# Tying the loads of the next tile's token blocks to the products on PE in a fused attention and FFN kernel

## The chip, the cores and the metric

The kernel runs on one core of a Trainium2 chip. The metric is the device time of one execution in microseconds. Five engines work in parallel, each through its own instruction list in order: PE (matrix products; its weight loads are shown as PEld), DVE and ACT (elementwise work), POOL (elementwise work too), and SP, which here only issues DMA transfers (SPq is its queue in the profile).

## The reference

```python
def reference(**kwargs):                       # B=4, H=8, S=576, D=64
    ...
    attn_out = _attn_ref(**attn_kwargs)        # softmax(q k_lm) Z softmax(q_lm k) v, 32 landmarks
    x = np.ascontiguousarray(attn_out.transpose(0, 2, 1, 3)).reshape(B * S, H * D)
    x = _moe_ref(x=x, **moe_kwargs)
    return _moe2_ref(x=x, **moe2_kwargs)

def _moe_ref(x, w_in, w_out):                  # 2304 x 512 -> 2048 -> 512
    h = x @ w_in
    relu6 = np.clip(h + 3.0, 0.0, 6.0)
    return (h * relu6 / 6.0 @ w_out).astype(np.float32)

def _moe2_ref(x, w_in, w_out):                 # 2304 x 512 -> 2048 -> 512
    h = x @ w_in
    g = np.where(h > 0.0, h, np.exp(np.minimum(h, 0.0)) - 1.0)
    return (g @ w_out).astype(np.float32)
```

A Nyström attention gives 2304 tokens of 512 values; two feed-forward layers follow. All is float32. The kernel splits each float32 operand into a high part (a cast to fp32r) and a low part (the rest), and adds three products on PE for each product of the reference. Splitting costs a cast on ACT and a subtraction on DVE or POOL; `to_pair` (line 308) does both.

## The kernel before

**Stages.** Attention and the first layer run together, in a loop over slots (`for i in range(END, NA)`). The first layer's output goes to DRAM as `x1d` (stores `x1d<-xs`). The second layer then works on three tiles of 768 tokens. Each tile runs eight steps (`for q in range(NTT * NQ)`, line 1460; 24 steps in all, q = 0 to 23), so tile 1 is q = 8 to 15 and tile 2 is q = 16 to 23.

**A step.** One step computes two blocks of 128 hidden rows for the tile's two blocks of 384 tokens, with seven block products in place of eight (`quartet`, line 1073). Each of the seven runs six products `h<-x,wi` into one of two banks, which DVE or ACT drains (`a1`, `u2`, `y`, `u3`); behind each come five or six products `x<-w,gh` and `x<-w,gl` of the step before (`second`, line 1128), which apply the output weights. Between them stand the ELU on ACT and DVE (`elu`, line 1049; `gf`) and the split of its result into `gh` (ACT) and `gl` (DVE); `ghl` is the name of such a pair in a buffer of another kind.

**The blocks of tokens.** The seven products want seven sums and differences of the tile's token blocks, for each of two halves (`kk`). `load_x` (line 992) makes them: for each half four DMA loads of 128x384 (192 KB) from `x1d` (line 1013), then eleven subtractions, of which seven belong to a split, with seven casts on ACT. Both tiles 1 and 2 do this on POOL: 8 loads, 14 casts and 22 subtractions each. It is a generator, and the loop takes one piece of it at each of the seven block places of a step (`next(xs, None)`). It starts at step q = 4 of the tile before (`XPACE`, lines 103 and 1464): tile 1's at q = 4, tile 2's at q = 12. Nothing but data and buffers holds these loads, and the scheduler places an instruction as soon as its inputs and its place are free; in the trace tile 1's loads and subtractions run from the last slots to q = 1.

**The weights.** In tile 0, `load_in2` loads the input weights of each step as written (`wi<-wi2d`, `u<-wi2d`), makes three sums of them on DVE (`u<-u,wi` and `u<-wi,u`, four instructions for a half, eight for a step) and splits them with ACT and POOL (`wi<-wi`, `wi<-u,wi`); the result is also stored (`wi2p<-wi`), and the tiles 1 and 2 load it ready from there. `load_out2` does the like with the output weights (`w<-wo2d`, split on ACT and POOL, stored by `wo2p<-w`).

**What sets the order.** A scheduler of the framework lays the instructions of all engines out by a priority (`wanted`, line 157, the smaller first) and by its own timeline of when inputs are ready. Products of the second layer go through `bmm` (line 1031), which chains each to the one before, so their order is as written; `chain[0]` is the last one placed. `gated` (line 170) ties an instruction behind the instruction in `gate[0]` (line 168), where one is set: an edge in the scheduler's order only, with no semaphore. SP's list is one queue for all loads and stores.

Of the kernel before, what the change touches and what calls it, by code (L numbers as in the profile page):

```python
# [31 lines left out]
def nystrom_ffn_kernel(ctx: ExitStack, tc, q, k, v, w_in1, w_out1, w_in2, w_out2, out):  # L32
# [46 lines left out]
    T2 = 384  # L79
# [44 lines left out]
    def after(inst, other):  # L124

        tc.add_manual_dep(
            inst.ins, other.name, mybir.DependencyInfo(mybir.DependencyClass.NoSync, mybir.DependencyReason.DATA)
        )

    vec, act, pool, pe = InOrder(nc.vector), InOrder(nc.scalar), InOrder(nc.gpsimd), InOrder(nc.tensor)  # L130
    sp = InOrder(nc.sync, False)

    def sub(o, a, b, eng=vec):
        return eng.tensor_tensor(out=o, in0=a, in1=b, op=ALU.subtract)
# [22 lines left out]
    def wanted(s):  # L157
        tc.cur_priority = int(1000 * (s + 100))
# [9 lines left out]
    gate = [None]  # L168

    def gated(inst):  # L170
        if gate[0] is not None:
            after(inst, gate[0])
# [17 lines left out]
    x1d = dram.tile([NDM, 128, NT], F32, name="x1d")  # L190
# [59 lines left out]
    def run(gen):  # L250
        for _ in gen:
            pass
# [55 lines left out]
    def to_pair(f, h, l, eng=vec):  # L308
        act.copy(out=h, in_=f)
        sub(l, f, h.bitcast(F32), eng)  # L310
# [54 lines left out]
    def scratch(n, w):  # L365

        return room().bitcast(F32).rearrange("p n t -> p (n t)")[:, 0:n * w].rearrange("p (a n) -> p a n", a=n)
# [8 lines left out]
    def sums_out2(q):  # L376

        a, b, c, d = (spare_x(4 * q + i).rearrange("p (j n) -> p j n", j=2) for i in range(4))
        for i, y in enumerate((b, a)):
            sp.dma_start(out=y, in_=wo2d[q + i * NQ].rearrange("p (j n) -> p j n", j=2))  # L380
        yield
        sub(c[:, 0], a[:, 1], a[:, 0], pool)
        sub(c[:, 1], b[:, 1], c[:, 0], pool)
        sub(d[:, 0], b[:, 1], a[:, 1], pool)
        sub(d[:, 1], c[:, 1], b[:, 0], pool)
        yield
        for x, y in ((a, c), (b, d)):
            to_pair(y, x.bitcast(F32R), y.bitcast(F32R), pool)
        yield
        o = q % 2 * HDM  # L390
        for j, ys in enumerate(((a, c), (b, d))):
            for x, y in enumerate(ys):
                sp.dma_start(out=to2p[2 * j:2 * j + 2, q // 2, x, :, o:o + HDM].rearrange("j p n -> p j n"), in_=y)
        yield
# [37 lines left out]
    def load_out2(q):  # L432

        if q // NQ in WINO:
            load_wino2(q)
            return
        for i in range(2):
            kk = q % NQ + i * NQ
            t = w2_place()
            hl = t.bitcast(F32R)  # L440
            if q < NQ:
                l = t[:, 1, :]
                sp.dma_start(out=l, in_=wo2d[kk])
                to_pair(l, hl[:, 0, :], hl[:, 1, :], pool)
                late_out.append((wo2p[kk].rearrange("x p n -> p x n"), t))
            else:
                sp.dma_start(out=t, in_=wo2p[kk].rearrange("x p n -> p x n"))
            wo2[q, i] = hl[:, 0, :], hl[:, 1, :]

    def load_in2(q):  # L450

        stores = late_out[:]
        late_out.clear()
        for kk in range(2):
            hl = []
            for x in range(2):
                if q % 2 == 0:
                    hl.append(win[0].tile([128, 7, 128], F32, name="wi", tag=f"wi{kk}{x}"))
                else:
                    t = nat.tile([128, G, W], F32, name="wi", tag=f"n{'hl'[x]}{kk}")  # L460
                    hl.append(t.rearrange("p g w -> p (g w)")[:, 0:7 * 128].rearrange("p (a n) -> p a n", a=7))
            h, l = hl
            hr, lr = h.bitcast(F32R), l.bitcast(F32R)
            wi[q, kk] = hr, lr
            flat = [x.rearrange("p a n -> p (a n)") for x in hl]
            if q >= NQ:
                for x in range(2):
                    sp.dma_start(out=flat[x], in_=wi2p[q % NQ, kk, x])
                continue
            f = scratch(4, 128)  # L470
            sp.dma_start(out=f[:, 0], in_=wi2d[q, kk][:, 3 * 128:])
            sp.dma_start(out=flat[1][:, 0:3 * 128], in_=wi2d[q, kk][:, 0:3 * 128])
            if kk:
                for o, i in stores:
                    sp.dma_start(out=o, in_=i)
                stores = []
            vec.tensor_tensor(out=f[:, 1], in0=f[:, 0], in1=l[:, 2], op=ALU.add)
            sub(f[:, 2], f[:, 1], l[:, 0])
            sub(f[:, 3], l[:, 1], f[:, 2])
            sub(f[:, 0], l[:, 0], f[:, 0])  # L480
            act.copy(out=hr[:, 0:3], in_=l[:, 0:3])
            sub(lr[:, 0:3], l[:, 0:3], h[:, 0:3], pool)
            act.copy(out=hr[:, 3:7], in_=f)
            sub(lr[:, 3:7], f, h[:, 3:7], pool)
            for x in range(2):
                late_out.append((wi2p[q, kk, x], flat[x]))
        for o, i in stores:
            sp.dma_start(out=o, in_=i)
# [490 lines left out]
    def x_places(t, n=14):  # L979

        for i in range(n):
            if t % 2 == 0:
                x = xp[0].tile([128, 2, T2], F32, name="x2", tag=f"x2{i}")
                yield x[:, 0], x[:, 1]
            elif NS + i < len(PLACES):
                x = wop.tile([128, 2, DM], F32, name="x2", tag=PLACES[NS + i])
                yield x[:, 0, 0:T2], x[:, 1, 0:T2]
            else:
                x = nat.tile([128, G, W], F32, name="x2", tag="nl3")
                yield x[:, 0, 0:T2], x[:, 1, 0:T2]  # L990

    def load_x(t, eng):

        places = x_places(t)
        t0 = 2 * T2 * t
        for kk in range(2):
            x = [next(places) for _ in range(7)]
            h, l = [y[0] for y in x], [y[1] for y in x]

            def pair(i, f):  # L1000
                xt_t[t, kk, i] = h[i].bitcast(F32R), l[i].bitcast(F32R)
                to_pair(f, *xt_t[t, kk, i], eng)

            if t:
                f = [
                    nat.tile([128, G, HALF], F32, name="xf", tag=n).rearrange("p g t -> p (g t)")[:, 0:T2]
                    for n in ("ath0", "ath1", "atl0")
                ]
            else:
                f = scratch(2, T2)  # L1010
                f = [f[:, 0], f[:, 1], scratch(1, T2)[:, 0]]
            for o, r, c in ((f[0], 0, 1), (l[0], 0, 0), (l[2], 1, 1), (l[1], 1, 0)):
                sp.dma_start(out=o, in_=x1d[2 * r + kk, :, t0 + c * T2:t0 + c * T2 + T2])
            yield
            sub(f[1], f[0], l[0], eng)
            yield
            sub(f[0], l[2], f[0], eng)
            yield
            sub(f[2], l[2], f[1], eng)
            yield  # L1020
            pair(5, f[0])
            yield
            sub(f[0], l[1], f[2], eng)
            yield
            for i, g in ((3, f[1]), (4, f[2]), (6, f[0]), (0, l[0]), (1, l[1]), (2, l[2])):
                pair(i, g)
                yield

    chain = [None]
# [380 lines left out]
    for i in range(END, NA):  # L1410
        b, r = i // SB, i % SB
# [48 lines left out]
    for q in range(NTT * NQ):  # L1460
        wanted(NA + 4 * q - 2)
        if q:
            load_in2(q + 1) if q + 1 < NTT * NQ else None
        if q % NQ == XPACE and q // NQ + 1 < NTT:
            xs = load_x(q // NQ + 1, pool)
        steps_ = quartet(q)
        if q == (WINO[0] - 1) * NQ:
            more = (None for r in range(NQ) for _ in sums_out2(r))
        for p in range(7):
            if p == 2:  # L1470
                load_out2(q)
            wanted(NA + 4 * q + 4 * p / 7 + 4)
            if conv and p % 2 == 0:
                conv.pop(0)()
            if p == 4 and q % NQ == NQ - 2 and q // NQ in WINO:
                load_late2(q // NQ, 0)
                load_late2(q // NQ, 1)
            next(more, None)
            next(xs, None)
            wanted(NA + 4 * q + 4 * p / 7)  # L1480
            next(steps_)
            for _ in range(2):
                next(tail, None)
            while n < (7 * q + p + 1 - 7 - LAG) * 12 * NS2 // 7:
                next(behind)
                n += 1
        run(steps_)
# [37 lines left out]
```

## Time and profile before

| what | value |
|---|---|
| time, median of 3 runs | 820.44 us (818.43 to 821.87) |
| the profiled execution | 818.11 us |
| its span | 816.3 us |
| PE busy | 782.2 us, 96% of the span |
| DVE busy | 539.4 us, 66% |
| ACT busy | 465.4 us, 57% |
| POOL busy | 416.2 us, 51% |
| DMA | 226 GB/s on average |

The span is the time from the first to the last instruction in the profile; the execution's own time is 1.8 us longer. Busy times are sums over the span, and the engines overlap. A wait shown in brackets behind an instruction is the idle time of its engine just before it, and the instruction that ended it. PEclk is the granted clock of PE as a share of 2.4 GHz.

### The profile page before, as it was taken

The numbers are of one execution on the slowest core, as the hardware profiler recorded it, in microseconds if no ns is written. First come the engines' busy times: TensorE is split into PE (matmuls) and PEld (weight loads), VectorE is DVE, ScalarE is ACT, GpSimd is POOL, SyncE is SP. The second block draws the span as 40 slices with busy tenths as digits, with TensorE's granted clock in tenths as the row PEclk, the third lists the DMA queues.
The fourth block names the chain that finished last, engine by engine and source line by source line (L and its number), as shares of the span: only waits on it lengthen the run. The fifth ranks groups of instructions, "written<-read, shape, count | busy, mean of one in ns | idle before, by whom it ended". The sixth has DMA issues, their size and how long they took to land.

```text
span 816.3 us, 16233 instructions
## 1 busy us (share of the span) xinstructions
PE 782.2 (96%) x5860; PEld 695.6 (85%) x5860; DVE 539.4 (66%) x1076; ACT 465.4 (57%) x1020; POOL 416.2 (51%) x423
## 2 busy tenths in 40 slices
PE   5699989999999999999998999999999999999998
PEld 3476777688997889889998899998999889999998
DVE  7899677557645754486346766756745565777794
ACT  3587554656656656584556556646644544555562
POOL 2567566556655665455428664539662470223311
PEclk9699999999999999999999999999999999999999
DMA  9967932685577445752352477689999567867663
GB/s 323 404 189 250 311 116 71 194 270 190 199 231 260 160 143 160 244 194 101 111 197 81 169 265 259 238 305 331 386 390 344 184 223 252 275 237 256 227 195 108
DMA packets 115599, 184.56 MB, mean 226 GB/s; under 512 B 8576, under 2 KB 71552, under 8 KB 115520
## 3 DMA queue, kind: packets, MB, share of 16 engines
q1 hardware_dynamic: 115520, 183.54, 65.9%
q8 instruction: 46, 0.75, 0.4%
q14 instruction: 33, 0.27, 0.1%
HBM read 130.02 MB, written 53.48 MB: 225 GB/s over the span
## 4 chain that ended last, share of the span: by engine, by line
PE 77%; DVE 11%; DMA 5%; ACT 3%; issue 2%; POOL 1%; DVEq 0%; ACTq 0%; POOLq 0%; SPq 0%
PE x L116 40%; PE h L116 31%; PE bk L116 6%; DVE u L116 2%; DVE h L116 1%; DVE lm L116 1%; DMA kt<-in_k 1%; DVE nl L116 1%; DMA qt<-in_q 1%; DVE w1c L116 1%; DVE st L116 1%; DVE gf L116 1%; DMA w1d<-w1c 1%; DVE y L116 1%; DMA u<-in_moe_w_in 1%
## 5 line engine op out<-in xcount | busy, mean ns | idle before, releaser
L116 PE MATMUL h<-x,wi 128*128 128x384 f32 x1008 | 205.4, 339 | 0.6 <-DVE u L116 0.6
L116 PE MATMUL x<-gh,wo 128*128 128x288 f32 (+1 forms) x896 | 198.5, 297 | 0.4 <-DVE wo L116 0.3
L116 PEld LDWEIGHTS h<-x,wi 128*128 128x128 f32 x1008 | 178.9, 189 | 10.4 <-DVE u L116 1.0
L116 PEld LDWEIGHTS x<-gh,wo 128*128 128x128 f32 x896 | 149.1, 188 | 10.3 <-issue 7.2
L116 PE MATMUL x<-gl,wo 128*128 128x288 f32 (+1 forms) x448 | 130.6, 294 | 0.0
L116 POOL TENSOR_TENSOR gl<-gf,gh 128x288 fp32r<-128x288 f32 (+1 forms) x100 | 83.9, 841 | 86.3 <-ACT gh L116 69.2
L116 ACT CAST gh<-gf 128x288 fp32r<-128x288 f32 (+2 forms) x160 | 72.5, 454 | 86.2 <-DVE gf L116 85.7
L116 PE MATMUL x<-w,gh 128*128 128x512 f32 (+1 forms) x360 | 102.4, 357 | 1.0 <-ACT gh L116 1.0
L116 ACT ACTIVATE gf<-h,half_b 128x288 f32<-128x288 f32 (+2 forms) x128 | 63.7, 500 | 42.6 <-PE h L116 40.5
L116 PE MATMUL h<-atl,nh 128*128 128x288 f32 (+2 forms) x256 | 81.9, 320 | 4.6 <-DVE gf L116 2.6
L116 DVE SCALAR_TENSOR_TENSOR gf<-gf,h 128x288 f32<-128x288 f32 (+1 forms) x112 | 49.4, 442 | 54.3 <-ACT gf L116 53.5
L116 PEld LDWEIGHTS x<-gl,wo 128*128 128x128 f32 x448 | 84.2, 188 | 1.1 <-issue 0.9
L116 DVE SCALAR_TENSOR_TENSOR gf<-gf,y 128x384 f32<-128x384 f32 x80 | 61.2, 765 | 32.9 <-ACT gf L116 32.9
L116 ACT ACTIVATE gf<-y 128x384 f32<-128x384 f32 x80 | 42.0, 525 | 62.5 <-DVE y L116 62.4
L116 PE MATMUL x<-w,ghl 128*128 128x512 f32 (+1 forms) x324 | 76.6, 356 | 0.1
L116 PE MATMUL h<-ath,nl 128*128 128x288 f32 (+2 forms) x256 | 76.5, 299 | 0.0
L116 PE MATMUL h<-ath,nh 128*128 128x288 f32 (+2 forms) x256 | 76.3, 298 | 0.0
L116 PEld LDWEIGHTS x<-w,gh 128*128 128x128 f32 x360 | 65.1, 190 | 7.4 <-ACT gh L116 1.4
L116 PE MATMUL x<-w,gl 128*128 128x512 f32 (+1 forms) x180 | 64.6, 359 | 3.6 <-DVE gl L116 3.6
L116 PEld LDWEIGHTS h<-atl,nh 128*128 128x128 f32 x256 | 48.5, 190 | 17.8 <-issue 7.9
L116 POOL TENSOR_TENSOR x<-u,gf 128x384 f32<-128x384 f32 x16 | 18.1, 1151 | 84.6 <-DVE gf L116 50.9
L116 PEld LDWEIGHTS x<-w,ghl 128*128 128x128 f32 x324 | 55.2, 189 | 5.8 <-DVE ghl L116 0.3
(183 smaller groups left out, 1520.6 us busy)
## 6 DMA issues: line engine op xcount, KB each, us to landing
wi<-wi2p SPq DMA_DIRECT2D x64, 448.0 KB, 5.8
wi2p<-wi SPq DMA_DIRECT2D x32, 448.0 KB, 2.9
u<-in_moe_w_in SPq DMA_DIRECT2D x25, 512.0 KB, 4.4
w1c<-w1d SPq DMA_DIRECT2D x48, 256.0 KB, 4.5
w<-wo2p SPq DMA_DIRECT2D x24, 512.0 KB, 7.0
ub<-in_moe_w_out SPq DMA_DIRECT2D x16, 512.0 KB, 10.2
u<-in_moe_w_out SPq DMA_DIRECT2D x16, 512.0 KB, 5.6
wo2p<-w SPq DMA_DIRECT2D x16, 512.0 KB, 3.6
```

The costliest lines, as they stand in the source:

```text
L116: inst = getattr(self.eng, name)(*a, **kw)
```

## The change

The four loads of each half of a tile are passed to `gated`. The loop sets `gate[0]` to the last product placed on PE (`chain[0]`) while it takes the next piece of `load_x`, and clears it again. The first call of `load_x` (for tile 0) is taken elsewhere, with no gate, and stays as it was.

```diff
@@ -1010,7 +1010,7 @@
             for o, r, c in ((f[0], 0, 1), (l[0], 0, 0), (l[2], 1, 1), (l[1], 1, 0)):
-                sp.dma_start(out=o, in_=x1d[2 * r + kk, :, t0 + c * T2:t0 + c * T2 + T2])
+                gated(sp.dma_start(out=o, in_=x1d[2 * r + kk, :, t0 + c * T2:t0 + c * T2 + T2]))
             yield
@@ -1476,7 +1476,9 @@
             next(more, None)
+            gate[0] = chain[0]
             next(xs, None)
+            gate[0] = None
             wanted(NA + 4 * q + 4 * p / 7)
```

No instruction is added or taken away; the scheduler puts some in other places. Three places matter below.

POOL at the start of the second layer, q = 0 and 1. The names `x2_65..` and `xf_65..` are the first half of tile 1's token blocks, `x2_68..` and `xf_68..` the second; `wi_5972` and `wi_5985` are the input weights that are split for q = 2:

```order
-L116 TENSOR_TENSOR x2_6815<-xf_6820,x2_6815 128x384
-L116 TENSOR_TENSOR x2_6814<-x2_6814 128x384
 L116 TENSOR_TENSOR wi_5972<-wi_5972,wi_5971 128x384
-L116 TENSOR_TENSOR x2_6817<-xf_6819,x2_6817 128x384
+L116 TENSOR_TENSOR wi_5972<-u_5973,wi_5971 128x512
 L116 TENSOR_TENSOR wi_5985<-wi_5985,wi_5984 128x384
-L116 TENSOR_TENSOR x2_6816<-xf_6821,x2_6816 128x384
-L116 TENSOR_TENSOR wi_5972<-u_5973,wi_5971 128x512
 L116 TENSOR_TENSOR wi_5985<-u_5986,wi_5984 128x512
-L116 TENSOR_TENSOR xf_6819<-x2_6813,xf_6821 128x384
-L116 TENSOR_TENSOR x2_6813<-x2_6813 128x384
-L116 TENSOR_TENSOR x2_6818<-xf_6819,x2_6818 128x384
```

All 22 subtractions of tile 1 leave this stretch, those above and 16 ahead of them; the four of `wi` now stand in a row. On DVE nothing changes up to the first `gl` of q = 1.

SP at q = 4. `w_6374` and `w_6378` are the output weights that are split for q = 3, the `wi` loads are for q = 5:

```order
 L116 DMA wo2p<-w_6374 128x2x512
 L116 DMA wo2p<-w_6378 128x2x512
+L116 DMA xf<-x1d 128x384
+L116 DMA x_6513<-x1d 128x384
+L116 DMA x_6515<-x1d 128x384
+L116 DMA x_6514<-x1d 128x384
 L116 DMA wi<-wi2d 128x384 x2
 L116 DMA w_6558<-wo2d 128x512
```

The four loads of the first half now go between the stores of the output weights and the loads of the next input weights. The four of the second half go, one by one, between stores of weights some two steps later.

POOL at the same place, q = 4; `wi_6482` and `wi_6495` are the input weights for q = 5:

```order
 L116 TENSOR_TENSOR w2_6378<-w2_6378 128x512
+L116 TENSOR_TENSOR xf_6521<-xf_6520,x2_6513 128x384
+L116 TENSOR_TENSOR xf_6520<-x2_6515,xf_6520 128x384
+L116 TENSOR_TENSOR xf_6522<-x2_6515,xf_6521 128x384
+L116 TENSOR_TENSOR x2_6513<-x2_6513 128x384
+L116 TENSOR_TENSOR x2_6516<-xf_6521,x2_6516 128x384
 L116 TENSOR_TENSOR wi_6482<-wi_6482,wi_6481 128x384
+L116 TENSOR_TENSOR x2_6515<-x2_6515 128x384
+L116 TENSOR_TENSOR x2_6518<-xf_6520,x2_6518 128x384
 L116 TENSOR_TENSOR wi_6495<-wi_6495,wi_6494 128x384
 L116 TENSOR_TENSOR wi_6482<-u_6483,wi_6481 128x512
+L116 TENSOR_TENSOR x2_6517<-xf_6522,x2_6517 128x384
```

Five subtractions stand ahead of the splits of `wi` here, and three among them. On ACT the casts of these blocks stand among the casts and exponentials of the same step, four of them ahead of the copy `a1` that drains the step's first bank.

POOL at q = 6, for the second half:

```order
 L116 TENSOR_TENSOR w2_6745<-w2_6745 128x512
+L116 TENSOR_TENSOR xf_6820<-xf_6819,x2_6812 128x384
+L116 TENSOR_TENSOR x2_6812<-x2_6812 128x384
+L116 TENSOR_TENSOR x2_6815<-xf_6820,x2_6815 128x384
+L116 TENSOR_TENSOR xf_6819<-x2_6814,xf_6819 128x384
+L116 TENSOR_TENSOR xf_6821<-x2_6814,xf_6820 128x384
+L116 TENSOR_TENSOR x2_6814<-x2_6814 128x384
+L116 TENSOR_TENSOR x2_6817<-xf_6819,x2_6817 128x384
+L116 TENSOR_TENSOR x2_6816<-xf_6821,x2_6816 128x384
+L116 TENSOR_TENSOR xf_6819<-x2_6813,xf_6821 128x384
 L116 TENSOR_TENSOR wi_6870<-wi_6870,wi_6869 128x384
```

Nine subtractions stand in a row ahead of the splits of the input weights for the step q = 7.

## Rows read from the trace of the kernel before

**Rows 1.** Part 1 of the page: busy us, share of the span, instructions.
```profile
PE 782.2 (96%) x5860; PEld 695.6 (85%) x5860; DVE 539.4 (66%) x1076; ACT 465.4 (57%) x1020; POOL 416.2 (51%) x423
```
**Rows 2.** Waits of PE, 200 to 452, then to 700: us in total, times, longest.
```profile
PE h L116 <- DVE gf L116: 2.6, 3, 1.2
...
PE h L116 <- DVE u L116: 0.6, 1, 0.6
```
**Rows 3.** Timeline of PE, 440 to 452: start, us, instruction, idle before and releaser.
```profile
445.49 0.74 PE L116 MATMUL x<-w,gh 128*128 128x512 f32 x2 [0.99 <-ACT gh L116]
...
450.87 0.53 PE L116 MATMUL x<-w,gl 128*128 128x512 f32 x1 [3.59 <-DVE gl L116]
```
**Rows 4.** Windows: us, PE, PEld, DVE, ACT, POOL busy, PEclk, DMA share, GB/s.
```profile
350.00:400.00 50.00, 47.31 (x353) 46.39 (x352) 30.21 (x55) 30.08 (x71) 26.81 (x28) 1.00 0.37 126
400.00:430.00 30.00, 30.00 (x228) 30.00 (x227) 14.78 (x32) 16.61 (x38) 11.51 (x11) 1.00 0.58 199
452.00:454.00 2.00, 2.00 (x7) 1.81 (x7) 1.43 (x3) 1.92 (x4) 2.00 (x2) 0.50 0.35 138
454.00:456.00 2.00, 2.00 (x9) 1.73 (x8) 1.26 (x2) 0.00 (x0) 2.00 (x3) 0.73 0.23 91
```
**Rows 5.** Chain that ended last, 450 to 472: start, us, work.
```profile
450.87 1.91 PE x L116 x5
...
454.70 1.39 PE x L116 x5
...
457.15 1.14 PE x L116 x5
...
468.40 1.14 PE x L116 x5
...
470.61 1.14 PE x L116 x5
```
**Rows 6.** Timeline of DVE, 440 to 452 and 492 to 504.
```profile
444.16 1.95 DVE L116 TENSOR_TENSOR u<-u,wi 128x128 f32<-128x128 f32 x2
...
449.47 1.35 DVE L116 TENSOR_TENSOR gl<-gf,gh 128x384 fp32r<-128x384 f32 x1
...
496.10 0.48 DVE L116 TENSOR_TENSOR u<-wi,u 128x128 f32<-128x128 f32 x2
```
**Rows 7.** Groups of DVE, 442 to 452, then 476 to 556: busy us, mean ns.
```profile
L116 DVE TENSOR_TENSOR u<-u,wi 128x128 f32<-128x128 f32 x4 | 3.3, 817 | 0.1
...
L116 DVE TENSOR_TENSOR u<-u,wi 128x128 f32<-128x128 f32 x16 | 4.3, 289 | 3.7 <-DMA wi<-wi2d 3.7
```
**Rows 8.** Groups of POOL, 427 to 464: the subtractions of tile 1's blocks.
```profile
L116 POOL TENSOR_TENSOR x<-xf,x 128x384 fp32r<-128x384 f32 x8 | 9.2, 1154 | 2.6 <-DVE y L116 2.5 <-ACT x L116 0.2
L116 POOL TENSOR_TENSOR x<-x 128x384 fp32r<-128x384 f32 x6 | 6.6, 1098 | 0.2
L116 POOL TENSOR_TENSOR xf<-x,xf 128x384 f32<-128x384 f32 x6 | 6.6, 1106 | 0.2
...
L116 POOL TENSOR_TENSOR xf<-xf,x 128x384 f32<-128x384 f32 x2 | 2.4, 1223 | 11.7 <-PE h L116 9.3 <-DMA xf<-x1d 2.5
```
**Rows 9.** Timelines: ACT at 444.93, SP's queue at 488.
```profile
444.93 0.51 ACT L116 CAST gh<-gf 128x384 fp32r<-128x384 f32 x1
...
488.11 1.88 SPq L116 DMA_DIRECT2D wo2p<-w  x2
```
**Rows 10.** DMA issues: count, KB each, median us to landing.
```profile
x<-x1d SPq DMA_DIRECT2D x18, 192.0 KB, 4.7
```
**Rows 11.** Waits of POOL, 476 to 550: us in total, times, longest.
```profile
POOL wi L116 <- DVE u L116: 28.4, 4, 7.5
```
**Rows 12.** Timelines of PE and DVE, 496 to 502.
```profile
496.27 1.23 PE L116 MATMUL h<-x,wi 128*128 128x384 f32 x6
...
498.48 0.54 DVE L116 TENSOR_TENSOR u<-h,a 128x384 f32<-128x384 f32 x1
...
500.68 1.23 PE L116 MATMUL h<-x,wi 128*128 128x384 f32 x6
```

## The prediction

> **What bounds the kernel now.** I read the page first, then who waited for whom on PE, then the stretch around PE's longest wait. PE is busy 782.2 of 816.3 us [rows 1], so an edit that touches neither PE's work nor its waits costs nothing. The products on PE are the same in number. What can change is PE's waits. Between 200 us and the end the waits are few: some of up to 1.2 us on DVE [rows 2], and two close together, 0.99 us before 445.49 and 3.59 us before 450.87 [rows 3]. They lie where the loop over quartets begins (step q = 1). Behind them the granted clock fell to 0.50 and 0.73 of 2.4 GHz for two 2 us slices, while it stayed at 1.00 over the stretch that holds the waits of up to 1.2 us [rows 4]. So the clock's cost is read from the chain: x5 and the h block behind it (11 products) start 3.83 us apart from 450.87 to 454.70 and 2.45 us from there to 457.15, against 2.21 us later (468.40 to 470.61) [rows 5]. That is 1.62 + 0.24 = 1.9 us. The place costs 0.99 + 3.59 + 1.9 = 6.5 us in all, and this is the most that the change can give.
>
> Why PE waited there: the second wait is for gl, which stands on DVE behind the splits of wi (u<-u,wi and u<-wi,u). Two of these took 1.95 us from 444.16, and gl itself 1.35 us [rows 6]. The same two take 0.48 us at 496.10 [rows 6]; by groups u<-u,wi takes 817 ns on average from 442 to 452 us and 289 ns from 476 to 556 [rows 7]. What differs is POOL: from 427 to 464 us it ran the 22 subtractions of the tile 1 blocks, 9.2 + 6.6 + 6.6 + 2.4 = 24.8 us [rows 8], and each DVE split got in only between two of them. The first wait is ACT's: gh was cast at 444.93 [rows 9], behind a cast of x and one of the newly loaded wi in its queue.
>
> By the Trainium skill (SBUF — State Buffer, "Who interferes with whom") a DVE instruction with two inputs in SBUF contends with a GpSimd instruction that reads SBUF, and whoever issues first takes the shared port for its whole length while the other blocks. The trace agrees: the splits have two SBUF inputs and read 817 against 289 ns. That rule speaks against this change as much as for it, since the subtractions are only moved; what it would do at the new place is the third rival below.
>
> **The change part by part.** No instruction is added or removed, and no semaphore wait: the edge only sets the place in SP's queue. There are 16 loads, eight for each of the tiles 1 and 2.
>
> Tile 1, out of the old place. Eight loads of 192 KB leave SP's queue ahead of the first quartets, 14 casts leave ACT, 22 subtractions leave POOL. On DVE the order up to gl is the same. The wi load stays where it was, behind the third store of xs, so the splits still begin at about 444.16: I leave 0.5 us of the first wait. With POOL empty until then, two splits take 0.48 us. Ahead of gl stand seven splits and one drain of an h bank (0.54 us, as u<-h,a in [rows 12]): 444.16 + 7 x 0.24 + 0.54 = 446.4 us, and even with the 1.35 us of before gl is there at 447.7. PE comes to it at 450.87 - 3.59 = 447.28. The wait is then 0 to 0.5 us, and I leave 0.2. So 4.6 - 0.7 = 3.9 us of waits go, and without a long wait the clock should not fall: 1.9 us. Together **-5.8 us**. The next late thing would be the wi load, at 0.5 us.
>
> The PE order also changes at five steps of the last slots (an h block goes ahead of two to six products of x). PE is busy for all of 400 to 430 us [rows 4], the inputs of both are there, and I take 0.
>
> Tile 1, into the new place. The first four loads now go behind the two stores of w of q = 3, issued by 489.99 us [rows 9], and land some 4.7 us later [rows 10], just as the splits for the next quartet run (496.10 [rows 6]). POOL has room in sum: its waits for DVE in 476 to 550 us are 28.4 us [rows 11], against 24.8 us of work. But what decides is not POOL's sum, it is DVE's delay. PE has two h buffers, so the block that begins at 500.68 needs the one of 496.27 drained, and DVE drains it (u<-h,a) from 498.48 to 499.02, behind the eight splits [rows 12]. The slack is 500.68 - 499.02 = 1.66 us. A held split costs (1.95 - 0.48) / 2 = 0.74 us more. Five subtractions stand ahead of the wi work in POOL's queue; with the first under way before wi has landed, I let four splits meet them: 4 x 0.74 - 1.66 = 1.3 us, and 0.4 us for ACT, on which four of the casts now stand ahead of a1 and the exponentials, the first waiting for its DMA. That is +1.7 us at q = 4.
>
> At q = 5 three subtractions follow: 3 x 0.74 = 2.2 us, within 1.66 + 1.7 of slack (PE is already late): 0. At q = 6 nine stand in a row, and the load of wi is now behind a store that waits for POOL. In the new DVE order five splits stand ahead of the drain: 5 x 0.74 - 1.66 = 2.0 us; part of this was paid at q = 4, so I take +1.7. Bounds of these two terms together: 0 from below (28.4 us of idle POOL take all of it, the splits fall between two subtractions), and from above every split held in three quartets, 3 x (8 x 0.74 - 1.66) = 12.8 us. A gain at this place is excluded: PE does not wait at all there. I take **+3.4 us**, nearer the lower end, because the subtractions also wait for ACT's casts, and splits slip in then.
>
> Tile 2. The same loads go behind the products of q = 12 to 15. There wi comes ready from DRAM and no split runs on DVE. PE waits once between 452 and 700 us, for 0.6 us, before these loads in before [rows 2]. The second half's loads stand earlier behind the first half's, and end earlier. I take 0, up to +1.
>
> Sum: -5.8 + 3.4 = **-2.4 us**. The profiled execution took 818.11 us, span and 1.8 us around it; that gives 815.7. The median of the runs, 820.44, is 2.3 above it, so I forecast 820.44 - 2.4 = **818.0 us**. Two medians of this kernel can tell 0.5%, or 4.1 us, from no change.
>
> **The rivals.** First: the new place hides all of it (POOL's idle 28.4 us). Then -5.8: 814.6 us, 814 with the rest of the 6.5 us. For it: one sum that fits easily; against it: the first five subtractions fall on the splits by the order. Second: the old wait stays. gl remains behind the splits, which start with the wi load, and if landing and not POOL set it, only some 1 us goes and the clock falls still; with the 3.4 us: 822.8 us. Against it: the row of 1.95 us, which begins when wi has landed. That the loads do not go where the words say is ruled out by the order, so I give it no chance of its own. Third, the slower one: DVE becomes the bound at q = 4 to 6. Here all eight splits of each of three quartets are held by POOL, which runs almost without a gap (its idle time at DVE in these quartets, 28.4 us, is about the 24.8 us of the new work). The price is 12.8 - 5.8 = +7.0, 827.4 us; it is slower than before from 5.8 us of lost slack on, that is when more than six of eight splits are held in two of the three. If each stop also lets the clock fall, 1.9 us more for each.
>
> By the rule of the Trainium skill cited above (SBUF — State Buffer) this third case is what an unbroken run on POOL gives; no row shows splits beside subtractions in the steady part of the loop.
>
> **How the numbers follow.** Forecast (a loss of 1.5 to 5 us): 0.46. First rival: 0.26. Second: 0.16. Third: 0.12. The forecast's own spread is 816.3 to 819.7. The range takes in the first two rivals and the noise of the runs (818.43 to 821.87): 813.8 to 823.6. Faster by over 0.5% needs under 816.3 us: nearly all of the first rival and a sixth of the forecast, 0.30. Slower by over 0.5%, above 824.5: the third rival and a little of the second, 0.13. Within 0.5%: 0.57.
>
> **What would show it.** In the profile of the changed kernel: the splits at 444 us at some 0.28 us each; PE's wait for gl under 0.5 us, and the clock at 1.00 from 440 to 460 us; the quartet q = 2 beginning some 6 us earlier. Then xf and x subtractions on POOL from some 488 to 540 us, splits there of 0.8 us, and PE waits for u (DVE) of 1 to 2 us at the fourth h block of q = 4 and q = 6. Wrong would be the prediction if the wait for gl is still over 2 us (the load set it), if PE does not wait at all from 480 to 545 us, or if it waits there more than 6 us.

## The result and the profile after

The changed kernel takes **825.29 us** (median; 824.39 to 827.30) against 819.68 us for the kernel before on the same chips (five runs each; the 820.44 us above is the median of three of those five). The ratio is 1.0066 (95% interval 1.0044 to 1.0087): slower by some 5.6 us. 818.0 us was forecast, in a range up to 823.6; it lies outside, and on the other side of no change.

The page of the kernel after, part 1, beside [rows 1]:

```profile
PE 783.3 (95%) x5860; PEld 694.7 (84%) x5860; DVE 545.6 (66%) x1076; ACT 463.7 (56%) x1020; POOL 413.2 (50%) x423
```

PE's work is what it was; its busy time is 1.1 us longer, the span of the profile 7.2 us (823.5 against 816.3). The waits of PE in the kernel after, from 430 to 452 us and then to 700 us (us in total, times, longest), beside [rows 2, 3]:

```profile
PE x L116 <- DVE gl L116: 0.7, 1, 0.7
...
PE h L116 <- DVE u L116: 6.4, 3, 2.7
PE h L116 <- DVE y L116: 1.1, 1, 1.1
PE h L116 <- ACT a L116: 0.8, 1, 0.8
```

The 0.99 + 3.59 us of q = 1 have become 0.7. In their place stand 8.3 us at q = 4 and q = 6, all on the drains of the two h banks.

How much each step cost is read from PE's timeline: the time from the first product of a step (the first `h<-x,wi` of its seven blocks) to that of the next. From q = 9 on, the two kernels agree within 0.01 us in every step. The stretch ahead of q = 0 is left out: its end lies at 429.36 us before, at 431.68 us after, and between 428.2 and 433.1 us in the profiles of the other kernels below. The difference is there already at PE's 2400th product (273.0 us before, 275.9 after), where PE's order is still the same in both; from the 3600th product to the start of q = 1, which holds the five steps with another order on PE, PE takes 30.12 us before and 30.13 after.

| us per step | q=1 | 2 | 3 | 4 | 5 | 6 | 7 | 8 | sum against before |
|---|---|---|---|---|---|---|---|---|---|
| before | 21.00 | 15.67 | 15.63 | 15.67 | 15.63 | 15.67 | 15.63 | 16.60 | |
| after | 15.57 | 16.01 | 15.64 | 21.26 | 15.63 | 21.27 | 15.64 | 15.71 | +5.2 |

So -5.4 at q = 1, +0.3 at q = 2, **+5.6 at q = 4, +5.6 at q = 6**, -0.9 at q = 8 (of that, a wait of 0.58 us on DVE's `u`, the only one of before between 452 and 700 us, is gone). The sum is the 5.6 us of the medians to within 0.4.

**The old place** went as forecast. DVE's timeline in the kernel after, beside [rows 6]:

```profile
445.87 0.62 DVE L116 TENSOR_TENSOR u<-u,wi 128x128 f32<-128x128 f32 x2 [0.34 <-issue]
446.41 0.28 DVE L116 TENSOR_TENSOR u<-wi,u 128x128 f32<-128x128 f32 x1
...
447.92 1.36 DVE L116 TENSOR_TENSOR gl<-gf,gh 128x384 fp32r<-128x384 f32 x1
449.21 1.38 DVE L116 TENSOR_TENSOR u<-wi,u 128x128 f32<-128x128 f32 x1
```

The splits take 0.28 us while POOL is idle. At 447.83 POOL begins its own `wi` work, and `gl` and the last split take 1.36 and 1.38 us: `gl` is still held, now by work that POOL did before as well.

**The new place.** PE, DVE, ACT and POOL of the kernel after around q = 4, whose first product starts at 491.06 (start, us, instruction, idle before and releaser):

```profile
496.63 1.31 PE L116 MATMUL h<-x,wi 128*128 128x384 f32 x6 [0.78 <-ACT a L116]
...
501.83 1.91 PE L116 MATMUL h<-x,wi 128*128 128x384 f32 x6 [2.72 <-DVE u L116]
```
```profile
493.75 0.58 DVE L116 TENSOR_TENSOR ghl<-gf,ghl 128x384 fp32r<-128x384 f32 x1 [2.96 <-ACT ghl L116]
494.75 1.63 DVE L116 TENSOR_TENSOR u<-u,wi 128x128 f32<-128x128 f32 x2 [0.42 <-DMA wi<-wi2d]
496.30 1.09 DVE L116 TENSOR_TENSOR u<-wi,u 128x128 f32<-128x128 f32 x1
497.32 1.10 DVE L116 TENSOR_TENSOR u<-u,wi 128x128 f32<-128x128 f32 x1
498.35 0.28 DVE L116 TENSOR_TENSOR u<-wi,u 128x128 f32<-128x128 f32 x1
498.55 0.28 DVE L116 TENSOR_TENSOR u<-u,wi 128x128 f32<-128x128 f32 x1
498.75 1.28 DVE L116 TENSOR_TENSOR u<-wi,u 128x128 f32<-128x128 f32 x2
499.96 1.34 DVE L116 SCALAR_TENSOR_TENSOR gf<-gf,y 128x384 f32<-128x384 f32 x1
501.23 0.54 DVE L116 TENSOR_TENSOR u<-h,a 128x384 f32<-128x384 f32 x1
```
```profile
492.90 1.02 POOL L116 TENSOR_TENSOR xf<-xf,x 128x384 f32<-128x384 f32 x1 [5.78 <-DMA x<-x1d]
494.00 2.23 POOL L116 TENSOR_TENSOR xf<-x,xf 128x384 f32<-128x384 f32 x2
496.19 1.06 POOL L116 TENSOR_TENSOR x<-x 128x384 fp32r<-128x384 f32 x1
497.21 1.07 POOL L116 TENSOR_TENSOR x<-xf,x 128x384 fp32r<-128x384 f32 x1
498.86 1.03 POOL L116 TENSOR_TENSOR wi<-wi 128x384 fp32r<-128x384 f32 x1 [0.58 <-DVE u L116]
```
```profile
492.79 0.52 ACT L116 CAST x<-x 128x384 fp32r<-128x384 f32 x1 [3.06 <-DMA x<-x1d]
493.21 0.51 ACT L116 CAST ghl<-gf 128x384 fp32r<-128x384 f32 x1
...
496.12 0.46 ACT L116 COPY a<-h 128x384 f32<-128x384 f32 x1
```

DVE's timeline of the kernel before has the first split of this step, whose first product starts at 493.83:

```profile
494.80 0.29 DVE L116 TENSOR_TENSOR u<-u,wi 128x128 f32<-128x128 f32 x1 [0.72 <-DMA wi<-wi2d]
```

Read DVE's and POOL's lines side by side. Four splits run beside the five subtractions, each as long as what is left of a subtraction. In POOL's gap from 498.28 to 498.86 the next two take 0.28 us again. With the next POOL instructions the last split and `gf` are long once more. The drain `u<-h,a`, which has one operand in PSUM and one in SBUF, takes 0.54 us in all of this, as in [rows 12]; but it stands behind them, and PE waits 2.72 us for it. ACT shows the second thing: it stood 3.06 us on a cast of `x` that waited for its DMA, and `a1` came late (0.78 us on PE). The cast of `ghl` stood behind that same cast, and DVE stood 2.96 us on `ghl`, which is ahead of the splits in its list. DVE was free at 494.33 us; it then waited 0.42 us more for `wi`, which came late as well. So two things held the first split almost equally long.

The chain of the kernel after shows a third, the clock (start, us, what):

```profile
501.83 1.91 PE h L116 x6
503.74 2.12 PE x L116 x5
505.86 1.05 PE h L116 x6
506.91 1.16 PE x L116 x5
```

The block and the five products behind the wait take 4.03 us, the next ones 2.21. The granted clock was 0.58 and 0.57 in the two slices from 502 to 506 us. So q = 4 is 0.78 + 2.72 + 1.82 = 5.3 of its 5.6 us. At q = 6 PE's waits are 2.56, 1.13 and 1.09 us; the clock stays at 1.00 there.

### The profile page after: what moved, and what is told of

The parts are those of the page before. It is cut to its first block, busy times and chain, and to the rows that moved or that the text cites. A ratio compares the mean times of both kernels' runs of the same rounds, so it can differ in the third digit from the quotient of the medians.

```text
span 823.5 us, 16234 instructions
## 1 busy us (share of the span) xinstructions
PE 783.3 (95%) x5860; PEld 694.7 (84%) x5860; DVE 545.6 (66%) x1076; ACT 463.7 (56%) x1020; POOL 413.2 (50%) x423
## 4 chain that ended last, share of the span: by engine, by line
PE 64%; DVE 15%; DMA 10%; ACT 5%; issue 3%; POOL 2%; SPq 1%; DVEq 0%; ACTq 0%; POOLq 0%
PE x L116 33%; PE h L116 26%; PE bk L116 5%; DVE u L116 3%; DMA u<-in_moe_w_in 2%; DMA u<-in_moe_w_out 2%; DVE h L116 2%; DMA wi<-wi2d 1%; DVE gf L116 1%; DVE nl L116 1%; DVE w1c L116 1%; DMA kt<-in_k 1%; DVE y L116 1%; DMA x<-x1d 1%; ACT gf L116 1%
## 5 line engine op out<-in xcount | busy, mean ns | idle before, releaser
L116 DVE SCALAR_TENSOR_TENSOR gf<-gf,y 128x384 f32<-128x384 f32 x80 | 65.5, 819 | 35.8 <-ACT gf L116 35.6
```

The source lines that it names most:

```text
L116: inst = getattr(self.eng, name)(*a, **kw)
```

## The experiments

Each kernel is named by its label. "Before" was timed beside each. The steps are read from the profile of each as above.

**t2only**, the gate for tile 2 alone:

```diff
-            gate[0] = chain[0]
+            gate[0] = chain[0] if q >= NQ else None
```

> The gate is set for tile 2's loads only; tile 1's loads run free as before. Whole change measured: 825.3 against 819.7 us. Theory A (POOL's subtractions hold DVE's two-input instructions, at q = 4 and q = 6 of tile 0) and theory B (casts that wait for their DMA at the head of ACT's list delay the drains there) both say that all of the change lies in tile 1: 819.7 us, within 1 us of before, and the wait of 3.6 us for gl near 450 us is back. If tile 2's gate had a share, the time would be over 821 or under 818.

Ratio 1.0016 (0.9993 to 1.0039), 820.43 us. The waits at q = 1 are back, 0.97 and 3.59 us, and no step from q = 2 to 7 differs from before. The whole change lies in tile 1.

**dve1**, the changed kernel with tile 1's 22 subtractions on DVE:

```diff
-            xs = load_x(q // NQ + 1, pool)
+            xs = load_x(q // NQ + 1, pool if q >= NQ else vec)
```

> The changed kernel, with the 22 subtractions of tile 1's blocks on DVE in place of POOL; loads and ACT casts stay gated as they are. Theory A: nothing on POOL holds the splits any more; DVE gets 22 x 0.55 = 12 us of work, and PE's waits at q = 4 and 6 (8.3 us in the trace after) fall to under 3: 815 to 819 us. Theory B: the casts and their DMA waits are the same, so the waits stay over 6 us: 823 to 826 us.

Ratio 1.0011 (0.9985 to 1.0037), 820.18 us: 5 us better than the change. q = 6 falls from 21.27 to 16.83, but q = 4 stays at 20.63. Neither theory's range holds the time: PE's waits at q = 4 and 6 come to 3.7 us, where A has under 3 and B over 6. DVE's timeline of dve1 at q = 4, and POOL's:

```profile
495.65 0.55 DVE L116 TENSOR_TENSOR x<-x 128x384 fp32r<-128x384 f32 x1
496.12 0.49 DVE L116 TENSOR_TENSOR u<-u,wi 128x128 f32<-128x128 f32 x2
...
499.20 1.53 DVE L116 TENSOR_TENSOR x<-xf,x 128x384 fp32r<-128x384 f32 x1
500.65 1.38 DVE L116 TENSOR_TENSOR u<-wi,u 128x128 f32<-128x128 f32 x1
```
```profile
499.01 2.86 POOL L116 TENSOR_TENSOR w<-w 128x512 fp32r<-128x512 f32 x2 [11.06 <-ACT w L116]
```

Until 499 us POOL is idle, and DVE's subtractions and splits take 0.55 and 0.25 us each. From the moment when POOL starts its work on `w`, both take 1.4 to 1.5 us. So it is not the subtraction as such: POOL's work on `w` does it too. But the first splits stood at 496.12 us, 4.4 us after the step's first product, against 1.0 before. Held splits don't explain that. In this trace the first split waits for nothing: DVE waited 1.73 us for the loads of `x` before it, and then had four of its own subtractions and a late `ghl` to do. What late `wi` does by itself is the question of loads4 and shift1.

**spread**, the changed kernel with tile 1's and tile 2's subtractions on POOL tied as the loads are (`gated` around each, while `next(xs)` runs).

> The changed kernel, with the subtractions on POOL also tied behind the product of their step, so that POOL takes at most a few of them in a row. Theory A: fewer splits are held at a time, some 4 to 6 us of the 11 us lost at q = 4 and 6 come back: 819 to 822 us, with waits of PE there of under 1.5 us each. Theory B: casts and loads hardly move, 824 to 826 us.

Ratio 1.0030 (1.0010 to 1.0051), 821.70 us. q = 4 takes 17.70, q = 5 18.51, q = 6 15.91, q = 7 17.27: the loss is shared out, and smaller.

**wipool**, the changed kernel with the eight sums and differences of `wi` on POOL:

```diff
-            vec.tensor_tensor(out=f[:, 1], in0=f[:, 0], in1=l[:, 2], op=ALU.add)
-            sub(f[:, 2], f[:, 1], l[:, 0])
+            pool.tensor_tensor(out=f[:, 1], in0=f[:, 0], in1=l[:, 2], op=ALU.add)
+            sub(f[:, 2], f[:, 1], l[:, 0], pool)
...
```

> The changed kernel, with the eight sums and differences of wi of each step of tile 0 on POOL in place of DVE. Theory A: DVE has no splits left that POOL could hold, the drains come in time: PE's waits at q = 4 and 6 under 3 us in all, no wait at q = 1, 814 to 818 us. Theory B: waits at q = 4 stay over 2.5 us, 822 to 826 us. A rival of its own: POOL, with 8 more instructions a step, becomes late with wi for the next step, and PE waits for wi at each step's first product: over 826 us.

Ratio 1.0139 (1.0095 to 1.0184), 830.35 us (four runs): its own rival came true, though at three steps and not at each. The waits of PE in wipool, 440 to 575 us:

```profile
PE h L116 <- POOL wi L116: 9.0, 3, 5.8
PE h L116 <- ACT a L116: 2.4, 3, 1.3
PE h L116 <- DVE u L116: 0.3, 1, 0.3
```

The waits on DVE's drains are gone (6.4 to 0.3 us), as theory A has it; `wi` for the next step comes late instead.

**half2**, only the second half's loads gated (`if kk: gated(inst)`):

> Only the second half's four loads of a tile are gated; the first half's loads and its 11 subtractions run free as before, ahead of the splits at q = 1. Theory A (POOL's subtractions beside DVE's two-input instructions): no split is held at q = 1 (-4.9 us there, as in the trace after), none at q = 4 (the 5.5 us lost there stay away), 11 subtractions still meet the splits at q = 6 (+5.5 us): 819 to 821 us, within 0.3% of before. If the loss at q = 6 only follows from PE being late at q = 4, it is under 2 us and the time 815 to 817 us. Theory B (casts waiting for their DMA at the head of ACT's list) gives the same sign but a wait on ACT's a1, not on DVE's u.

Ratio 1.0007 (0.9990 to 1.0025), 820.55 us. q = 1 takes 15.74, q = 4 15.67, q = 6 21.61. The loss of q = 6 stands by itself, it doesn't follow from q = 4: PE waits 2.93 us for `u` there, and the clock falls behind it. And the first half alone, run free, doesn't disturb q = 1.

**window**, the changed kernel with tile 1's pieces behind its first four loads only at the last four block places of q = 4 to 7, up to two at a place, casts and subtractions tied:

> The changed kernel; the pieces of tile 1 are taken only at the last four block places of the steps q = 4 to 7, two at a place, and casts and subtractions are tied behind their product as well, so that POOL runs them behind the splits of wi and not beside them. Theory A: the gain at q = 1 stays (-4.9 us), the loss at q = 4 to 7 falls from 11 to under 3 us: 815 to 818 us. Theory B: the casts no longer stand ahead of a1 either, so the time alone does not tell; by B alone the waits on DVE's u at q = 4 and 6 stay over 4 us and the time over 821.

Ratio 0.9997 (0.9980 to 1.0014), 820.24 us: worse than expected. The splits of q = 4 run free (0.28 us each), but PE waits 2.9 us for `y` in all. Timelines of DVE, POOL and ACT of window at the end of q = 4:

```profile
506.64 1.62 DVE L116 SCALAR_TENSOR_TENSOR gf<-gf,y 128x384 f32<-128x384 f32 x1 [3.46 <-ACT gf L116]
508.18 0.54 DVE L116 TENSOR_TENSOR y<-h,u 128x384 f32<-128x384 f32 x1
```
```profile
506.57 1.28 POOL L116 TENSOR_TENSOR w<-w 128x512 fp32r<-128x512 f32 x1
507.80 3.91 POOL L116 TENSOR_TENSOR x<-xf,x 128x384 fp32r<-128x384 f32 x3
```
```profile
505.67 0.52 ACT L116 CAST x<-xf 128x384 fp32r<-128x384 f32 x1 [2.40 <-POOL xf L116]
```

`gf` also has two operands in SBUF. Beside POOL it took 1.62 us in place of 0.55, and the drain `y` behind it was late. But it also began late: DVE stood 3.46 us on ACT's `gf` (0.69 at the like places of before), since ACT stood 2.40 us on a cast of `x` that waited for POOL. So it isn't enough to keep the splits clear: `gf` is held like them, and a cast of `x` that isn't ready holds all that ACT has behind it. The second is the larger part here.

**half2w**, the first half free as before, the second half as in window, at q = 5 and 6:

> As the run above, but the first half runs free as before and only the second half is tied and put behind the splits of q = 5 and 6. Theory A: -4.9 us at q = 1 (the first half ends before the splits begin), under 1.5 us lost at q = 5 to 7: 814 to 817 us, the best of the kernels here. If free subtractions of the first half still meet DVE's work at q = 0 and 1, the wait for gl is over 1.5 us and the time 817 to 820.

Ratio 0.9962 (0.9941 to 0.9982), 817.51 us, a little over what was expected: q = 5, 6 and 7 take 16.50, 17.04 and 16.21. The wait for `gl` is 0.8 us, so free subtractions at q = 0 and 1 are not the reason.

**half2e** and **half2d**, the first half free, the second half from q = 2 to 4, one piece at each of the last four block places; in half2d its subtractions are on DVE. Of half2e (the casts and subtractions of `load_x` go through `gated` while `held[0]`):

```diff
-        if q % NQ == XPACE and q // NQ + 1 < NTT:
+        if q in (1, NQ + XPACE):
...
-            gate[0] = chain[0]
-            next(xs, None)
-            gate[0] = None
+            gate[0] = None if (q, p) == (1, 0) else chain[0]
+            held[0] = q < NQ
+            for _ in range({(1, 0): 12, (1, 3): 1, (2, 3): 1, (2, 4): 1, (2, 5): 1, (2, 6): 1, (3, 3): 1, (3, 4): 1, (3, 5): 1, (3, 6): 1, (4, 3): 1, (4, 4): 1, (4, 5): 1}.get((q, p), 0) if q < NQ else 1):
+                next(xs, None)
+            gate[0], held[0] = None, False
```

> First half free as before; the second half's loads are tied behind q = 1, and its pieces are taken one at a block place, at the last four places of q = 2 to 4, subtractions on POOL. Theory A as it stands now (every stretch in which POOL runs without a gap holds DVE's instructions that read two operands from SBUF, gf and gl as well as the splits): the steps q = 1 to 4 take under 16.2 us each in the trace, 0.3 to 1.2 us lost in all against 5.1 gained: 814 to 817 us. If the cost goes with the number of subtractions and not with how densely they stand, it is as in the run before with two at a place, 2.8 us: 817 to 818 us.

> As the run above, with the second half's 11 subtractions on DVE in place of POOL. If DVE's own time decides (11 x 0.55 = 6 us over three steps, in which it is not full), nothing is lost: 814 to 816 us. If a DVE subtraction that meets POOL's wi and w is held like the others (1.4 to 1.6 us in the trace of the run with all of them on DVE), 0.5 to 1.5 us is lost in each step: 816 to 819 us.

half2e: ratio **0.9947 (0.9929 to 0.9964)**, 814.73 us, the best of all, and clear of both kernels. Its steps from q = 1 to 8 are 14.98, 16.32, 15.74, 15.66, 15.64, 15.66, 15.64 and 16.92 us. The number of subtractions can't be what decides, since half2w has as many. That it is the density of POOL's work fits, but isn't shown alone: from half2w to half2e the steps (q = 5 to 7, then q = 2 to 4) and the place of the loads change too. half2d: 0.9987 (0.9969 to 1.0005), 817.81 us; q = 2 takes 17.80 and q = 3 16.37: DVE's own subtractions are held by POOL's `wi` and `w`, as in dve1. The waits of PE in half2e, 452 to 575 us:

```profile
PE h L116 <- DVE u L116: 0.5, 1, 0.5
PE h L116 <- DVE y L116: 0.5, 1, 0.5
```

**castgate**, the changed kernel with tile 1's casts on ACT tied too:

> The changed kernel with tile 1's 14 casts on ACT also tied behind the product of their step; the subtractions are not tied, but each waits for its cast and so moves with it. Theory A and B both expect less than the 825 us of the change; A: POOL's runs of x subtractions at q = 4 get shorter (three in a row in place of five) and the wait for a1 goes: q = 4 takes under 18 us, but at q = 6 five still stand in a row: over 16.5 us; 818 to 822 us. B alone: both steps come down to 15.7 us, 815 us.

Ratio 1.0018 (0.9995 to 1.0040), 820.45 us; q = 4 takes 15.96, but q = 5, 6 and 7 take 17.34, 17.64 and 16.73. The subtractions move with their casts, and the loss moves with them; B alone, with 15.7 us for both steps and 815 us, did not come true. Its q = 4 shows one more thing, on DVE (the step starts at 491.40):

```profile
494.45 1.31 DVE L116 TENSOR_TENSOR u<-u,wi 128x128 f32<-128x128 f32 x2 [2.80 <-DMA wi<-wi2d]
```

The four loads still stand ahead of `wi`, and the first split begins 3.05 us after the step's start, on account of `wi` alone. No cast holds ACT ahead of it and only one split is held, and the step loses 0.3 us. So a `wi` late by 2 us costs little where nothing else is late before the same drain.

**loads4**, the kernel before (with t2only's gate) and four loads that nobody reads, where the change puts its own at q = 4; and **shift1**, the changed kernel with each piece of tile 1 one block place later:

```diff
+            if (q, p) == (4, 0):
+                gate[0] = chain[0]
+                for i in range(4):
+                    gated(sp.dma_start(out=dsp[i], in_=x1d[i, :, 0:T2]))
+                gate[0] = None
```
```diff
-            next(xs, None)
+            if (q, p) != (XPACE, 0):
+                next(xs, None)
```

> The kernel before (the gate of tile 2 stays, which moved nothing), plus four more loads of 192 KB from x1d into a spare DRAM buffer that nobody reads, put where the change puts its four loads at q = 4: in SP's queue between the stores of w and the loads of wi. No cast and no subtraction moves. Theory C, new: in the trace after, the splits at q = 4 begin 3.7 us after the step's first product, against 1.0 before, since wi stands behind the four loads; that is 2.7 of the 5.5 us by which the drain is late, the other 2.8 are the held splits. By C the splits begin 2.5 to 3.7 us after the step's start here too, the drain comes some 2 us late, and the step takes 15.7 to 16.7 us against 15.67 before. If the loads have no part (A alone), the splits begin at 1.0 us and the step takes 15.67. The time is within 1.5 us of before either way; the trace tells.

> The changed kernel with every piece of tile 1 taken one block place later, so that at q = 4 the first of wi's two loads goes ahead of all four x loads in SP's queue and the second behind one of them; on POOL one subtraction in place of five stands ahead of the splits' first consumer. Theories A and C together: the splits begin 1 to 2 us after the step's start, the step q = 4 takes 16 to 18.5 us in place of 21.3; q = 6 is moved by one place too and takes 16 to 21. In all 818 to 823 us. If neither held splits nor late wi cause the loss at q = 4, it stays over 20 us.

loads4 in time: 0.9998 (0.9981 to 1.0016), 820.54 us. Its step q = 4 takes 17.69 us, a loss of 2.0, with no subtraction there. SP's queue, then DVE and PE of loads4 (q = 4 starts at 495.81):

```profile
493.35 3.24 SPq L116 DMA_DIRECT2D dsp<-x1d  x4
496.69 1.01 SPq L116 DMA_DIRECT2D wi<-wi2d  x2
```
```profile
501.28 0.62 DVE L116 TENSOR_TENSOR u<-u,wi 128x128 f32<-128x128 f32 x2 [4.04 <-DMA wi<-wi2d]
```
```profile
502.24 1.32 PE L116 MATMUL h<-x,wi 128*128 128x384 f32 x6 [1.64 <-ACT a L116]
```

Four loads take SP 3.24 us to issue, and `wi` goes out and lands behind them; the splits begin 5.5 us after the step's start, later than in the kernel after (3.7), and the loads go to DRAM here, so the size is an upper one. PE's wait is for `a1`, which stood on ACT behind a cast of `wi`. In the kernel after, the same rows:

```profile
487.57 0.84 SPq L116 DMA_DIRECT2D xf<-x1d  x1
488.46 2.21 SPq L116 DMA_DIRECT2D x<-x1d  x3
490.77 0.85 SPq L116 DMA_DIRECT2D wi<-wi2d  x2
```

shift1: 1.0019 (1.0001 to 1.0036), 821.97 us. q = 4 falls to 16.49 as expected, with the splits at 1.1 us. q = 6 takes 17.80. Not expected: q = 5 takes 21.52, where it took 15.63. DVE's timeline of shift1 there:

```profile
509.38 2.13 DVE L116 TENSOR_TENSOR u<-u,wi 128x128 f32<-128x128 f32 x2
511.44 1.10 DVE L116 TENSOR_TENSOR u<-wi,u 128x128 f32<-128x128 f32 x1
```

The subtractions that were pushed back now meet the next step's splits. The first split begins 2.2 us after the step's start and waits for nothing, so `wi` is not late here, and this is what held instructions cost by themselves: 8.2 us from the first split to the drain against 3.8 before.

## Why the prediction was wrong, point by point

- **What bounds the kernel**: right. Only PE's waits moved the time.
- **Out of the old place, -5.8 us**: right in the waits, and in part a draw in size. The wait left for `gl` is 0.70 us (0.2 was left), that for `gh` is gone (0.5 was left), the clock stays at 1.00, and q = 1 is 5.4 us shorter. But t2only has the same two waits with the clock at 1.00, and its q = 1 takes 19.39 us; against that profile the gain is 3.8 us.
- **PE's order at five steps, 0, and tile 2, 0**: right. That stretch takes PE 30.12 and 30.13 us, and t2only, with tile 2 alone gated, is as before. The gain of 0.9 us at q = 8 had no term.
- **Into the new place, +3.4 us: the step that failed.** It measured 11.2, 5.6 at each of q = 4 and q = 6; 1.7 was taken for each. PE waited 7.2 us between 480 and 545 us, and more than 6 was the prediction's own sign of being wrong. What the term was made of, at q = 4:
  - The price of the held splits came out near, but by luck. From the first split to the drain it takes 6.5 us after and 3.7 before: 2.8 us more, where 4 x 0.74 = 3.0 was taken. But five splits and `gf` were held, which is 4.4 us more; 1.6 us of what stood between the first split and the drain before (`ghl` and two waits) now stood elsewhere.
  - The slack of 1.66 us was already spent. The sum let the splits start when they did before. They began 3.7 us after the step's first product, not 1.0, for two reasons side by side. The four loads stand ahead of `wi` in SP's queue: `wi` is issued 0.3 us ahead of the step's start, where it was 1.5, and lands 4.0 us later, where it was 2.5. The order shown with the change has those rows, and the prediction saw the loads land "just as the splits for the next quartet run"; no term had a price for what that does to `wi`. And ACT's cast of `x`, waiting for its load, held `ghl` and with it DVE until 494.33 us, 0.42 us ahead of the first split; the prediction gave ACT 0.4 us in all, for `a1` and the exponentials, and `a1` alone cost 0.78. loads4 shows that the loads alone can make the splits late, castgate that this costs only 0.3 us at q = 4 when little else is late. Together the drain is 2.7 + 2.8 = 5.5 us late.
  - A wait of 2.72 us let the clock fall: 1.8 us. The sum had it at the old place, and left it out at the new one.
- At q = 6 it is not late `wi`: the first split begins 4.2 us after the step's start and waits for nothing. DVE came to it behind a `gf` and a `ghl` that had waited for ACT and a second `gf` of 1.37 us, held by POOL. The drain follows at 9.0 us, and then come two more waits: 1.13 us for a drain behind two splits that took 2.67 us, 1.09 us for one behind a `gf` of 1.65. The three waits make 4.8 of the 5.6 us; the rest stays open. "Part of this was paid at q = 4" was wrong. half2 has no loss at q = 4 and loses 5.9 us at q = 6.
- **The third rival** was the nearest: it names DVE behind POOL as the bound. Its 12.8 us, every split held in three steps, were meant as the upper end, and the loss was 11.2 in two. The range stopped at 823.6, though the same text gave this case 827.4 and a chance of 0.12. POOL's idle time in sum, 28.4 us, on which the first rival and the lower bound rest, says nothing on when POOL is idle. (The forecast's own spread, by a loss of 1.5 to 5 us, is 816.1 to 819.6, not 816.3 to 819.7; nothing hangs on it.)
- The rule of the Trainium skill (SBUF — State Buffer, "Who interferes with whom"), that DVE instructions with two SBUF inputs contend with GpSimd's reads, and those with at most one, outside the 2-port perf modes, do not, agrees with what the runs show: the drain from PSUM takes 0.54 us beside a busy POOL, while splits, `gf`, `gl` and subtractions go from 0.28 or 0.55 us to 1.1 to 1.6. The same section says that DMA never contends with a compute engine; no run here tests that.

What stays open: how the 2.7 us by which the splits start late at q = 4 divide between `wi` and ACT's cast, since taking away either alone would have let them start at most 0.42 us earlier; and why `wi` lands 1.5 us slower, besides its issue 1.2 us later. No run separates these. Why q = 0 starts up to 5 us earlier or later from profile to profile is open too; the difference lies ahead of the places that the change moves.

## What to carry to other kernels

When work is moved, price every list that it joins: here four loads went in front of one that an in-order chain waits for, and casts that wait for those loads went in front of the step's own work on ACT. Both spent the slack before POOL held a single split. Then look at whether the other engine has gaps where the work lands, not at its idle time in sum; here the kernel with one subtraction at a block place lost almost nothing, and those with two at a place, or five to nine in a row, lost one to several microseconds, at other steps and with other loads beside them. Slack is to be spent once: list all that is late before the same drain, and add it up.

## What the runs showed of the hardware

A run of POOL without gaps slows DVE's instructions with two SBUF operands in time with it: splits of 0.28 us took 1.1, and 0.28 us again in a gap of 0.58 us between two of POOL's instructions.

The clock's fall behind a wait isn't certain. t2only has the two waits of before, 0.97 and 3.59 us; the windows behind (us, busy time of PE, PEld, DVE, ACT and POOL, granted clock, DMA share, GB/s), to be held against [rows 4]:

```profile
452.00:454.00 2.00, 2.00 (x11) 1.78 (x11) 1.83 (x4) 1.25 (x3) 1.72 (x2) 1.00 0.33 129
454.00:456.00 2.00, 2.00 (x12) 1.79 (x11) 1.76 (x3) 1.00 (x3) 2.00 (x3) 1.00 0.58 229
```

The granted clock stays at 1.00, and q = 1 takes 19.39 us in place of 21.00. At q = 6 it falls behind a wait of 2.93 us in half2, and not behind one of 2.56 us in the kernel after. A single profile's clock cost, here 1.6 to 1.9 us a stall, is one draw.
